# Holding back weights and second-batch transposes while the first scale is made, and six points per chunk in blocks of 256

## The chip, the cores and the metric

The kernel runs on one core of a Trainium2 chip. TensorE (PE) multiplies, VectorE (DVE) and ScalarE (ACT) work on tiles, GpSimd (POOL) does small side work, and SyncE (SP) issues nearly all transfers. The metric is the device time of one launch in microseconds (us), lower is better.

## The reference

Masked attention over 4 batches, 8 heads, 576 positions and head size 64, then two gated feed-forward layers over the 2304 tokens (512 wide, 1536 hidden). Heads 0 to 3 see the last 32 positions ("local"), heads 4 to 7 every 32nd earlier position ("strided").

```
attn = softmax(where(mask, q @ k.T / 8, -1e9)) @ v
x  = attn.transpose(0, 2, 1, 3).reshape(2304, 512)
xn = x / sqrt(mean(x * x, -1) + 1e-6) * rms_g        # layer 1 only
y  = (silu(xn @ w_gate) * (xn @ w_val)) @ w_out      # layer 1
out = (silu(y @ w2_gate) * (y @ w2_val)) @ w2_out    # layer 2
```

## The kernel before

**Products.** Each feed-forward operand is split into a high and a low part that TensorE multiplies in the type fp32r. A product of 128 by 128 weights with a token block is therefore three matmuls (high times high, high times low, low times high). The 1536 hidden columns are 12 chunks of 128. In layer 1 the first six chunks run over token blocks 0 (tokens 0 to 255), 1 (256 to 511), 2 (512 to 1023), 3 and 4; the last block of 256 tokens then runs all twelve chunks, and the others follow with chunks 6 to 11. Layer 2 goes the other way round. A chunk is a gate product (`b_g`), a value product (`b_v`), each 12 matmuls, and, two chunks later, the down product (`b_y`, 12 matmuls). While attention is still running there is one PSUM bank for the gate and one for the value (`GV`), so the gate product of a chunk can begin only when VectorE has read the one before it (`silu`, L670).

**Weights.** `weight_step` (L158) loads one of the three weights of a chunk (SP, L166), then rebuilds and splits it with three ScalarE and three VectorE instructions of 128x512: `dh` and `raw` on ScalarE (L175, L176), `raw` and `dh` on VectorE (L182, L183), `w` on ScalarE (L189) and `w` on VectorE (L194). The first six chunks have 18 weights. Three load buffers are shared with the loads of token blocks (`xraw`).

**Attention.** `Attention.batch` lists the steps of a batch: strided transposes (`strided_t`), scores with softmax, transposes of the softmax (`turn_step`), products with the values, local ones in the same way. From the second token block on they use two PSUM banks, `a0` and `a1`, in turn: a step's TensorE instructions wait until the bank's last reader on ScalarE or VectorE has finished.

**Normalising.** `rms_step(b, part)` scales a part of batch b: `pe1` sums squares on TensorE (`ones,ss`), `mean` runs on VectorE (L575) and then a power on GpSimd (L578), `diag` puts the result on a diagonal (`dg`, L583), `bc` spreads it over the partitions with TensorE (`dg,ones`), `post` scales x on VectorE (L594) and `store` writes x to DRAM. Batch 0's first part (256 tokens) is block 0: `split_x` (L693, L694) makes its high and low parts from SBUF. All later blocks come back from DRAM (`xraw`, L653) before their split. Block 2 needs the first part of batch 1.

**What sets the order.** One list of weight steps and one of attention steps are drawn from at "points" (`point`, L121), which stand between matmuls. At each point every active step moves on by one phase, and a new one starts when enough of its pace has gathered. In the start stage (up to batch 0's first part) there are only points; afterwards `proj` has points after its first and third quarter, `gate` one after each half and `down` two in layer 1: eight per chunk. A scheduler then places the instructions of each engine by priority; each engine executes its own in that order.

Of the kernel before, what the change touches and what calls it, by code (L numbers as in the profile page):

```python
# [8 lines left out]
F32 = mybir.dt.float32  # L9
# [3 lines left out]
ALU = mybir.AluOpType  # L13
# [8 lines left out]
PRIO_W = -150  # L22
# [3 lines left out]
def attn_ffn_ffn(ctx: ExitStack, tc: tile.TileContext, q, k, v, w1g, w1v, w1o, rms_g, w2g, w2v, w2o, out):  # L26
    nc = tc.nc
# [54 lines left out]
    last = {}  # L82
    active = []
    steps = []
    wq = []
    state = {"start": True, "rest": False, "kind": ""}

    def phase(st, prio=None):
        prio = st.prio if prio is None else prio
        with tc.high_priority(offset=0 if state["start"] and prio == PRIO_A else prio):  # L90
            state["kind"] = st.kind
            st.pop(0)()
            state["kind"] = ""

    def advance():
        for st in list(active):
            phase(st)
            if not st:
                active.remove(st)
# [21 lines left out]
    def point():  # L121
        advance()
        for nm, src in (("dec", wq), ("att", steps)):
            have[nm] = min(have[nm] + pace[nm], 2.0)
            while have[nm] >= 1.0 and src and src[0].ready():
                have[nm] -= 1.0
                start(src.pop(0))
# [80 lines left out]
    class Attention:  # L208
# [154 lines left out]
        def strided_t(self, b, which, part, last):  # L363
            cell = {}
            n = (126, 108, 108)[part]
            m = 64 if part == 2 else 128

            def pe():
                src = self.ld[b, 1][which]
                cell["t"] = tp = self.abank()  # L370
                for h in range(HH):
                    turned(tp[:m, n * h:n * h + n], src[:n, h, 128 * part:128 * part + m], self.ident[:n, :n])

            def post():
                o = (0, 504, 936)[part]
                copy(self.eng(), self.qk_tile(b, 1, which)[:m, o:o + 4 * n], cell["t"][:m, 0:4 * n])
                self.count(b, 1)
                if last:
                    self.load(b, 0)
                    if b == 0:  # L380
                        self.load_v(0, 0)

            return Step([pe, post])

        def softmax_step(self, ready, key, qn, kn, mks, mms):

# [171 lines left out]
        def rms_step(self, b, part):  # L558
            cell = {}
            o, w = parts(b)[part]  # L560
            tiles = [(j, min(128, w - j)) for j in range(0, w, 128)]
            nt = len(tiles)

            def pe1():
                cell["m"] = mp = self.abank()
                for i, (j, n) in enumerate(tiles):
                    product(mp[:n, i:i + 1], self.ss[b][:, o + j:o + j + n], self.ones[:, 0:1], start=True, stop=True)

            def mean():
                mp = cell["m"]  # L570
                m = self.p1.tile([128, 32], F32, tag="mean", name="mean")
                nc.gpsimd.memset(m, 1.0)
                for n in sorted({n for _, n in tiles}):
                    i0, i1 = [i for i, t in enumerate(tiles) if t[1] == n][0], [i for i, t in enumerate(tiles) if t[1] == n][-1] + 1
                    nc.vector.tensor_scalar(out=m[:n, i0:i1], in0=mp[:n, i0:i1], scalar1=1.0 / DM, scalar2=1e-6,  # L575
                                            op0=ALU.mult, op1=ALU.add)
                cell["r"] = r = self.p1.tile([128, 32], F32, tag="rstd", name="rstd")
                nc.gpsimd.tensor_tensor(out=r[:, :nt], in0=m[:, :nt], in1=self.expo[:, :nt], op=ALU.pow)  # L578

            def diag():  # L580
                cell["d"] = dg = self.p2.tile([128, 4, 128], F32, tag="e", name="dg", bufs=4).rearrange("p a k -> p (a k)")
                for i, (j, n) in enumerate(tiles):
                    nc.vector.tensor_scalar(out=dg[:n, j:j + n], in0=self.ident[:n, :n],  # L583
                                            scalar1=cell["r"][:n, i:i + 1], scalar2=None, op0=ALU.mult)

            def bc():
                cell["t"] = t = self.abank()
                for j, n in tiles:
                    product(t[:, j:j + n], self.ones[:n, :], cell["d"][:n, j:j + n], start=True, stop=True)

            def post():
                for c in range(KC):
                    x = self.x[b, c // 2][:, c % 2, o:o + w]
                    nc.vector.scalar_tensor_tensor(out=x, in0=x, scalar=self.gcol[:, c:c + 1], in1=cell["t"][:, :w],  # L594
                                                   op0=ALU.mult, op1=ALU.mult)

            def store():
                d = dp.tile([128, KC, w], F32, name=f"x_d{b}_{part}")
                for half in range(2):
                    nc.sync.dma_start(out=d[:, 2 * half:2 * half + 2, :], in_=self.x[b, half][:, :, o:o + w])  # L600
                x_d.append((b * S + o, w, d))
                self.done.add((b, part))

            return Step([wait] * 3 + [pe1, mean, diag] + [wait] * 1 + [bc, post, store], lambda: (b, part + 1) in self.sq and (not part or (b, 0) in self.done and not state["start"]), PRIO_R, "r")
# [57 lines left out]
    def ins_of(r):  # L662
        return getattr(r, "ins", r)
# [19 lines left out]
    @ahead  # L683
    def split_x(si):
        m, t0, n = segs[si][:3]
        xs = []
        x = xraw.pop((m, t0), None)
        p, w = pools[si % 2]
        for c in range(KC):
            xc = (x[c // 2] if x is not None else att.x[0, c // 2])[:, c % 2, :n]  # L690
            xh = p.tile([128, w], F32R, tag=f"xh{c}", name="xh")
            xl = p.tile([128, w], F32R, tag=f"xl{c}", name="xl")
            nc.scalar.copy(out=xh[:, :n], in_=xc)  # L693
            nc.vector.tensor_tensor(out=xl[:, :n], in0=xc, in1=xh[:, :n].bitcast(F32), op=ALU.subtract)  # L694
            xs.append((xh, xl))
        return xs

    def proj(pst, n, wtile, xs):
        for kk in range(KC):
            xh, xl = xs[kk]  # L700
            hi, lo = wtile[:, 0, kk * 128:kk * 128 + 128], wtile[:, 1, kk * 128:kk * 128 + 128]
            for a, b_, f, l in ((hi, xh, kk == 0, False), (hi, xl, False, False), (lo, xh, False, kk == KC - 1)):
                product(pst[:, :n], a, b_[:, :n], start=f, stop=l)
            if kk % 2 == 0:
                point()

    def gate(m, c, n, xs):
# [108 lines left out]
    waiting = []  # L816
    with tc.high_priority(offset=PRIO_R):
        xs_of = {0: split_x(0)}
    for _ in range(6):
        point()  # L820

# [17 lines left out]
    for si, (m, t0, n, c0, c1) in enumerate(segs):  # L839
        nxt = segs[si + 1] if si + 1 < len(segs) else None  # L840
        loaded = False
        pace["att"] = 0.6 if si < 2 else 1.2
        state["rest"] = si > TURN1
        pace["dec"] = 0.3 if si in (TURN1, TURN2) else 0.25
        xs = xs_of.pop(si)
# [59 lines left out]
```

## Time and profile before

| | us |
|---|---|
| median of 3 runs (1060.06 to 1067.89) | 1060.79 |
| profiled execution, time | 1059.67 |
| profiled execution, span | 1057.9 |
| PE busy / DVE busy / ACT busy / POOL busy | 1023.6 / 456.1 / 432.4 / 59.1 |

The profiled execution's time is 1.8 us more than its span. TensorE is busy for 97% of the span, so time can only come from the 34 us in which it is idle, from stretches where its granted clock is 1.2 instead of 2.4 GHz, and from waits that the busy time hides. In the page's forty slices the granted clock is at nine tenths or more in all but the second and the third.

### The profile page before, as it was taken

How to read it: one execution, taken by the hardware profiler on the slowest of the kernel's cores; microseconds unless marked ns; L12 is line 12 of the kernel's file. 1: busy time of each engine (PE TensorE's matmuls, PEld its weight loads, DVE VectorE, ACT ScalarE, POOL GpSimd, SP SyncE). 2: the span in 40 equal slices, each digit the busy share in tenths (PEclk: the TensorE clock that was granted, in tenths of full speed). 3: DMA queues.
4: the chain of work that ended last, by engine and by line, in shares of the span. 5: the costliest groups of instructions: out<-in, count | busy, mean ns of one | idle time of the engine just before them, and what ended most of it. 6: DMA issues, size and time to landing. Idle time of an engine off the chain costs nothing.

```text
span 1057.9 us, 14777 instructions
## 1 busy us (share of the span) xinstructions
PE 1023.6 (97%) x5624; PEld 865.8 (82%) x5624; DVE 456.1 (43%) x1104; ACT 432.4 (41%) x1046; POOL 59.1 (6%) x83
## 2 busy tenths in 40 slices
PE   5878999999999999999999999999999999999998
PEld 4667998787788899888888898888888888888887
DVE  3788364463447563751322785222224322222212
ACT  5988655465436463631211674212114322212111
POOL 3212112021000000000000000000000000000000
PEclk9759999999999999999999999999999999999999
DMA  7684161250135451741202474111103203020202
GB/s 194 186 229 141 40 188 46 77 155 2 41 110 186 142 169 39 216 142 54 99 21 80 140 229 160 40 40 40 40 1 120 80 1 99 11 80 1 80 1 90
DMA packets 100704, 100.71 MB, mean 95 GB/s; under 512 B 39445, under 2 KB 84701, under 8 KB 100633
## 3 DMA queue, kind: packets, MB, share of 16 engines
q1 hardware_dynamic: 100440, 99.49, 30.1%
q8 instruction: 44, 0.72, 0.3%
q0 software_dynamic: 192, 0.28, 0.1%
q14 instruction: 28, 0.22, 0.1%
HBM read 77.73 MB, written 22.02 MB: 94 GB/s over the span
## 4 chain that ended last, share of the span: by engine, by line
PE 89%; DVE 4%; DMA 3%; ACT 1%; SPq 1%; issue 1%; POOL 1%; DVEq 0%; POOLq 0%
PE b_y L66 28%; PE b_a L66 27%; PE b_v L66 16%; PE b_g L66 16%; PE b_a L69 2%; DMA raw<-in_moe_w_val_dram 1%; DVE e L399 1%; SPq L265 1%; DVE dh L183 1%; DMA raw<-in_moe_w_gate_dram 1%; DVE raw L182 1%; DMA kn<-in_k_dram 0%; DVE w L194 0%; DVE x L594 0%; DMA xraw<-y_d 0%
## 5 line engine op out<-in xcount | busy, mean ns | idle before, releaser
L66 PE MATMUL b_a<-xh,w 128*128 128x512 f32 (+1 forms) x816 | 234.8, 364 | 0.0
L66 PE MATMUL b_g<-xh,w 128*128 128x512 f32 (+1 forms) x600 | 182.1, 364 | 0.0
L66 PE MATMUL b_v<-xh,w 128*128 128x512 f32 (+1 forms) x600 | 180.9, 362 | 0.0
L66 PEld LDWEIGHTS b_a<-xh,w 128*128 128x128 f32 x816 | 147.9, 189 | 24.6
L680 ACT CAST hh<-sg 128x512 fp32r<-128x512 f32 (+1 forms) x126 | 70.3, 558 | 204.2 <-DVE sg L679 189.5
L66 PE MATMUL b_y<-hh,w 128*128 128x512 f32 (+1 forms) x528 | 153.0, 355 | 0.0
L66 PE MATMUL b_a<-xl,w 128*128 128x512 f32 (+1 forms) x408 | 148.5, 364 | 0.0
L66 PE MATMUL b_y<-w,hh 128*128 128x512 f32 x432 | 133.3, 390 | 0.0
L66 PEld LDWEIGHTS b_g<-xh,w 128*128 128x128 f32 x600 | 109.8, 190 | 17.1 <-issue 0.2
L66 PEld LDWEIGHTS b_v<-xh,w 128*128 128x128 f32 x600 | 108.9, 189 | 16.4
L66 PE MATMUL b_g<-xl,w 128*128 128x512 f32 (+1 forms) x300 | 107.1, 357 | 0.1
L66 PEld LDWEIGHTS b_y<-hh,w 128*128 128x128 f32 x528 | 95.0, 189 | 14.5 <-issue 0.7
L66 PE MATMUL b_v<-xl,w 128*128 128x512 f32 (+1 forms) x300 | 106.5, 355 | 0.0
L679 DVE TENSOR_TENSOR sg<-sg,b_v 128x512 f32<-128x512 f32 (+1 forms) x51 | 31.8, 623 | 162.6 <-PE b_v L66 162.4
L679 DVE TENSOR_TENSOR sg<-sg,b_a 128x512 f32<-128x512 f32 (+1 forms) x51 | 31.8, 623 | 157.8 <-PE b_a L66 157.7
L681 DVE TENSOR_TENSOR hl<-sg,hh 128x512 fp32r<-128x512 f32 (+1 forms) x126 | 79.3, 630 | 47.0 <-ACT hh L680 46.5
L66 PEld LDWEIGHTS b_y<-w,hh 128*128 128x128 f32 x432 | 80.4, 188 | 16.2
L66 PE MATMUL b_y<-hl,w 128*128 128x512 f32 (+1 forms) x264 | 92.6, 351 | 0.0
L66 PEld LDWEIGHTS b_a<-xl,w 128*128 128x128 f32 x408 | 77.0, 189 | 12.4
L672 ACT ACTIVATE sg<-b_a 128x512 f32<-128x512 f32 (+1 forms) x51 | 27.9, 547 | 140.9 <-PE b_a L66 140.7
L66 PE MATMUL b_y<-w,hl 128*128 128x512 f32 x216 | 84.0, 389 | 0.0
L672 ACT ACTIVATE sg<-b_g 128x512 f32<-128x512 f32 (+1 forms) x51 | 28.0, 548 | 120.8 <-PE b_g L66 120.7
(121 smaller groups left out, 1242.5 us busy)
## 6 DMA issues: line engine op xcount, KB each, us to landing
raw<-in_moe_w_gate_dram SPq DMA_DIRECT2D x24, 512.0 KB
raw<-in_moe_w_val_dram SPq DMA_DIRECT2D x24, 512.0 KB
raw<-in_moe_w_out_dram SPq DMA_DIRECT2D x24, 512.0 KB
xraw<-y_d SPq DMA_DIRECT2D x14, 512.0 KB
part<-ob SPq DMA_DIRECT2D x26, 256.0 KB
ob<-part SPq DMA_DIRECT2D x26, 256.0 KB
out_dram<-ob SPq DMA_DIRECT2D x18, 256.0 KB
y_d<-ob SPq DMA_DIRECT2D x16, 256.0 KB
```

The source lines that it names most:

```text
L66: traced(nc.tensor.matmul(out_, a, b_, start=start, stop=stop))
L69: traced(nc.tensor.transpose(out_, a, one))
L182: nc.vector.scalar_tensor_tensor(out=r, in0=cell["hw"], scalar=0x80000000, in1=r, op0=ALU.bitwise_and, op1=ALU.bitwise_or)
L183: nc.vector.scalar_tensor_tensor(out=h, in0=h, scalar=3, in1=r, op0=ALU.logical_shift_left, op1=ALU.bitwise_or)
L265: engs[h].dma_start(out=t[0:108, h].rearrange("p (g d) -> p g d", d=D), in_=s)
L399: r = nc.vector.tensor_tensor_reduce(out=e[:qn, i, :kn], in0=sp[:qn, i, :kn], in1=mk[:qn, :kn], scale=-0.125, scalar=3.0e38, op0=ALU.add, ...
L672: last["act"] = ins_of(nc.scalar.activation(out=s[:, :n], in_=pg[:, :n], func=AF.Silu))
L679: nc.vector.tensor_tensor(out=s[:, :n], in0=s[:, :n], in1=pv[:, :n], op=ALU.mult)
L680: last["act"] = ins_of(nc.scalar.copy(out=hh[:, :n], in_=s[:, :n]))
L681: last["dve"] = ins_of(nc.vector.tensor_tensor(out=hl[:, :n], in0=s[:, :n], in1=hh[:, :n].bitcast(F32), op=ALU.subtract))
```

## The change

Five edits. (1) While batch 0's first scale is being made, from its `pe1` to `split_x` of block 0, `hold` keeps weight steps from starting and from moving on. (2) The strided transposes of batch 1 become ready only when that part is done. (3) The first product after the start stage is ordered after the last one of `rms_step`. (4) Weight instructions of VectorE and ScalarE are placed behind the last split of block 0. (5) In blocks of 256 tokens `proj` has one point, after its second quarter, instead of two: a chunk then has six points (layer 1). The pace of attention in blocks 0 and 1 goes from 0.6 to 0.7 per point: 4.2 steps a chunk instead of 4.8. The pace of weights per point stays.

```diff
@@ state, advance, point @@
-    state = {"start": True, "rest": False, "kind": ""}
+    state = {"start": True, "hold": False, "rest": False, "kind": ""}
...
         for st in list(active):
+            if state["hold"] and st.prio == PRIO_W:
+                continue
             phase(st)
...
         for nm, src in (("dec", wq), ("att", steps)):
+            if state["hold"] and nm == "dec":
+                continue
@@ strided_t @@
-            return Step([pe, post])
+            return Step([pe, post], lambda: b != 1 or (0, 0) in self.done)
@@ rms_step, pe1 @@
+                if (b, part) == (0, 0):
+                    state["hold"] = True
@@ split_x @@
-            nc.scalar.copy(out=xh[:, :n], in_=xc)
-            nc.vector.tensor_tensor(out=xl[:, :n], in0=xc, in1=xh[:, :n].bitcast(F32), op=ALU.subtract)
+            ra = nc.scalar.copy(out=xh[:, :n], in_=xc)
+            rd = nc.vector.tensor_tensor(out=xl[:, :n], in0=xc, in1=xh[:, :n].bitcast(F32), op=ALU.subtract)
+            if si == 0:
+                last["act"], last["dve"] = ins_of(ra), ins_of(rd)
@@ proj @@
-            if kk % 2 == 0:
+            if kk in ((0, 2) if n > 256 else (1,)):
                 point()
@@ after the start stage @@
         xs_of = {0: split_x(0)}
+    state["hold"] = False
+    last["pe", None] = last["pe", "r"]
...
-        pace["att"] = 0.6 if si < 2 else 1.2
+        pace["att"] = 0.7 if si < 2 else 1.2
```

**TensorE, the first broadcast of the scale** (`dg,ones`) and the first transposes of batch 1 (`qn_482`, `kn_488`), as the difference of the two orders:

```order
 L66 MATMUL b_y_789<-ones,ss 128x1 x2
 L66 MATMUL b_a_809<-pT,vl_223 64x64 x4
+L66 MATMUL b_g<-dg,ones 128x128 x2
 L69 MATMUL b_a_860<-ident,qn_482 128x126 x4
 L69 MATMUL b_a_867<-ident,kn_488 128x126 x4
-L66 MATMUL b_g<-dg,ones 128x128 x2
 L69 MATMUL b_a_874<-ident,qn_482 128x108 x4
 L66 MATMUL b_a_879<-ones,ss 128x1 x2
```

The broadcast moved ahead of two groups of transposes. All six groups still stand ahead of the first gate product.

**VectorE, from the last squares to the second `mean`, before** (line 594 scales x, 694 splits it, 182, 183 and 194 are weight instructions):

```order
L555 TENSOR_TENSOR ss<-ss,sq 128x320
L183 SCALAR_TENSOR_TENSOR dh<-dh,raw 128x512
L594 SCALAR_TENSOR_TENSOR x_744<-x_744,gcol,b_g 128x256 x2
L594 SCALAR_TENSOR_TENSOR x_406<-x_406,gcol,b_g 128x256 x2
L182 SCALAR_TENSOR_TENSOR raw<-raw 128x512
L194 TENSOR_TENSOR w_3_1_500<-dh,w_3_1_500 128x512
L575 TENSOR_SCALAR mean<-b_a_879 64x1
L575 TENSOR_SCALAR mean<-b_a_879 128x2
```

The same place now (the line numbers of the changed kernel are 4 to 6 higher):

```order
L559 TENSOR_TENSOR ss<-ss,sq 128x320
L600 SCALAR_TENSOR_TENSOR x_744<-x_744,gcol,b_g 128x256 x2
L600 SCALAR_TENSOR_TENSOR x_406<-x_406,gcol,b_g 128x256 x2
L187 SCALAR_TENSOR_TENSOR dh<-dh,raw 128x512
L186 SCALAR_TENSOR_TENSOR raw<-raw 128x512
L700 TENSOR_TENSOR xl<-x_744,xh 128x256 x2
L700 TENSOR_TENSOR xl<-x_406,xh 128x256
L186 SCALAR_TENSOR_TENSOR raw<-raw 128x512
L187 SCALAR_TENSOR_TENSOR dh<-dh,raw 128x512
L581 TENSOR_SCALAR mean<-b_a_879 64x1
L581 TENSOR_SCALAR mean<-b_a_879 128x2
L700 TENSOR_TENSOR xl<-x_406,xh 128x256
```

One weight instruction moved from ahead of the scaling to behind it; the second `mean` now has four weight instructions and three splits between the scaling and itself, where it had two weight instructions.

**TensorE, the broadcast for block 2** (batch 1's first part) in block 1, before, where it stands between chunk 2 and the down product of chunk 0:

```order
L66 MATMUL b_v<-xl,w_2_1_435 128x256
L66 MATMUL b_v<-xh,w_2_1_435 128x256
L66 MATMUL b_a_1799<-dg,ones 128x128 x3
L66 MATMUL b_a_1799<-dg,ones 128x64
L66 MATMUL b_y_1804<-hh,w_0_2_281 128x256
```

and now, between the gate and the value product of chunk 4:

```order
L66 MATMUL b_g<-xl,w_4_0_556 128x256
L66 MATMUL b_g<-xh,w_4_0_556 128x256
L66 MATMUL b_a_1877<-dg,ones 128x128 x3
L66 MATMUL b_a_1877<-dg,ones 128x64
L66 MATMUL b_v<-xh,w_4_1_592 128x256
```

It moved back by nearly two of the six chunks of block 1. Between it and block 2's first product there are now 60 matmuls of 256 columns, six groups of transposes and batch 1's second broadcast.

## Rows read from the trace of the kernel before

**Rows 1.** The page's first line: the span of the profiled execution.

```profile
span 1057.9 us, 14777 instructions
```

**Rows 2.** Windows: start:end, length; busy PE, PEld, DVE, ACT, POOL; granted clock; DMA.

```profile
60.00:80.00 20.00, 17.44 (x100) 15.30 (x99) 18.70 (x57) 16.00 (x41) 4.08 (x4) 0.64 0.93 246
80.00:100.00 20.00, 16.15 (x132) 14.50 (x131) 17.91 (x60) 18.84 (x61) 6.93 (x6) 1.00 0.43 135
140.00:200.00 60.00, 59.12 (x470) 49.97 (x469) 28.85 (x134) 38.06 (x133) 11.25 (x13) 1.00 0.35 105
200.00:320.00 120.00, 119.51 (x706) 96.62 (x705) 57.22 (x187) 56.98 (x165) 14.10 (x18) 1.00 0.27 80
320.00:1057.00 737.00, 733.32 (x3572) 621.08 (x3570) 279.75 (x458) 235.69 (x428) 0.00 (x0) 1.00 0.26 85
```

**Rows 3.** Timeline of PE, 83 to 99: in brackets the idle time before.

```profile
83.43 0.65 PE L69 MATMUL b_a<-ident,e 126*126 126x126 f32 x4 [1.04 <-POOL e L425]
...
91.26 0.66 PE L69 MATMUL b_a<-ident,kn 128*128 128x128 f32 x4 [0.49 <-ACT x L76]
...
94.52 0.66 PE L69 MATMUL b_a<-ident,qn 128*128 128x128 f32 x4 [1.54 <-DVE qT L78]
...
98.18 0.33 PE L69 MATMUL b_a<-ident,qn 64*128 64x64 f32 x2 [0.78 <-DVE qT L78]
```

**Rows 4.** Timeline of PE, the first gate products and what stands before.

```profile
68.77 0.90 PE L69 MATMUL b_a<-ident,qn 108*64 108x108 f32 x4 [0.21 <-DVE mean L575]
...
70.39 0.56 PE L66 MATMUL b_g<-xh,w 128*128 128x256 f32 x1
...
72.46 1.71 PE L66 MATMUL b_a<-dg,ones 128*128 128x128 f32 x6
...
76.34 1.11 PE L66 MATMUL b_a<-kT,qT 64*126 64x126 f32 x8
```

**Rows 5.** Timeline of VectorE (DVE), 65 to 84.

```profile
65.03 0.69 DVE L183 SCALAR_TENSOR_TENSOR dh<-dh,raw 128x512 uint32<-128x512 uint32 x1
...
65.64 1.65 DVE L594 SCALAR_TENSOR_TENSOR x<-x,gcol,b_g 128x256 f32<-128x256 f32 x4
...
68.41 0.21 DVE L575 TENSOR_SCALAR mean<-b_a 64x1 f32<-64x1 f32 x2
...
70.42 0.74 DVE L694 TENSOR_TENSOR xl<-x,xh 128x256 fp32r<-128x256 f32 x2
...
71.92 0.64 DVE L583 TENSOR_SCALAR dg<-ident,rstd 128x128 f32<-128x128 f32 x3 [0.76 <-POOL rstd L578]
...
74.28 1.91 DVE L594 SCALAR_TENSOR_TENSOR x<-x,gcol,b_a 128x320 f32<-128x320 f32 x4
...
83.58 0.42 DVE L670 SCALAR_TENSOR_TENSOR sg<-sg,b_g 128x256 f32<-128x256 f32 x1
```

**Rows 6.** Timeline of GpSimd (POOL): two powers of the same shape.

```profile
68.77 3.12 POOL L578 TENSOR_TENSOR rstd<-mean,expo 128x3 f32<-128x3 f32 x1 [7.09 <-DVE mean L575]
...
206.40 0.86 POOL L578 TENSOR_TENSOR rstd<-mean,expo 128x3 f32<-128x3 f32 x1 [14.89 <-DVE mean L575]
```

**Rows 7.** Windows: the stretch up to block 0's last weight.

```profile
60.50:98.80 38.30, 31.89 (x215) 28.13 (x212) 34.92 (x113) 33.72 (x98) 11.01 (x10) 0.82 0.71 199
```

**Rows 8.** Timeline of VectorE: the last two weights of chunk 5.

```profile
98.16 1.29 DVE L194 TENSOR_TENSOR w<-dh,w 128x512 fp32r<-128x512 f32 x2
```

**Rows 9.** Chain of waits: start us, us, what: twelve products of 256 columns.

```profile
131.06 1.44 PE b_y L66 x12
```

**Rows 10.** Timeline of VectorE: two scalings, for blocks 2 and 3.

```profile
138.03 2.45 DVE L594 SCALAR_TENSOR_TENSOR x<-x,gcol,b_a 128x448 f32<-128x448 f32 x4 [0.58 <-PE b_a L66]
...
211.02 2.19 DVE L594 SCALAR_TENSOR_TENSOR x<-x,gcol,b_a 128x384 f32<-128x384 f32 x4
```

**Rows 11.** Timeline of ScalarE (ACT): the splits that follow them.

```profile
146.86 1.14 ACT L693 CAST xh<-xraw 128x512 fp32r<-128x512 f32 x2 [1.69 <-DMA xraw<-x_d]
...
217.93 1.14 ACT L693 CAST xh<-xraw 128x512 fp32r<-128x512 f32 x2 [0.85 <-DMA xraw<-x_d]
```

## The prediction

> **What bounds the kernel now.** I read the page first, then windows over stages, then TensorE's timeline where the windows leave it idle, and last the engines that it waits for there. The span is 1057.9 us [rows 1]. From 320 us to the end TensorE is idle for 3.7 us of 737 (737.00 less 733.32), from 200 to 320 for 0.49 of 120, from 140 to 200 for 0.88 of 60 [rows 2]: there the kernel is TensorE's own work, which the change leaves as it is. What an order can win lies between 60 and 100 us. There TensorE is idle for 2.56 and 3.85 us of two times 20, and its granted clock is 0.64 in the first of the two (a mix of the 1.2 and the 2.4 GHz level) [rows 2]. In the second the idle time is four gaps of 1.04, 0.49, 1.54 and 0.78 us [rows 3], 3.85 together. All four stand before a transpose of attention, whose operand or bank comes late from GpSimd, ScalarE or VectorE. The reader should see next that VectorE is busy for 34.92 of the 38.3 us up to the last weight of the first six chunks [rows 7]: in this stretch the bound is VectorE's queue, in its order, and TensorE waits for it.
>
> **The change part by part.**
>
> *The scale.* The broadcast now stands ahead of two groups of transposes, but the scaling of x on VectorE still comes behind the same squares and weight products; only one weight instruction (0.61 us, the step from 65.03 to 65.64) leaves the place ahead of it [rows 5]. So the scaling starts at 65.03 instead of 65.64, 0.6 us earlier, and nothing more is won on this path.
>
> *The second mean.* What VectorE puts between that scaling and the second `mean` grows: before, 2.77 us (65.64 to 68.41), namely the scaling and two weight instructions [rows 5]. Now it is the scaling (2.77 less two times 0.61, so 1.55), four weight instructions (2.44) and three splits of 0.37 (half of the 0.74 at 70.42), 1.11 [rows 5]: 5.10 us. The mean comes at 65.03 + 5.10 = 70.1 instead of 68.4, 1.7 us later. TensorE's fifth group of transposes waited for just this mean (0.21 us at 68.77), since it takes over its bank, and the first gate product followed at 70.39 [rows 4]. All transposes still stand ahead of it, so it starts at about 72.1. The edit that holds the weights back thus delays the gate by 1.7 us, by way of a bank.
>
> *The second scale.* It needs the power on GpSimd behind that mean. At 68.77 the power took 3.12 us, the same shape at 206.40 took 0.86 [rows 6]. At 68.77 VectorE ran on until 71.16 (70.42 + 0.74) and then waited 0.76 us for the power [rows 5]: it ended 0.73 us after VectorE's last instruction. I take that as the price: power done 0.73 us after VectorE pauses. Now a split and two weight products (1.6 us) follow the mean (70.1 + 0.2), so VectorE pauses at 71.9 and goes on at 72.6. The Trainium skill, GPSIMD Engine Reference, section Specifications, says that GpSimd shares its SBUF interfaces with VectorE and contends with VectorE instructions that have two SBUF inputs; by that rule, which speaks against placing such products behind the mean, the sum is the one above, and by a flat 3.12 us the second scale would come at 73.4 and the whole stretch 0.8 us later. The rows agree with the rule, as far as one power can.
>
> From 72.6 VectorE has the diagonal (0.64), four weight instructions (2.44), the gate's product (0.42), another weight instruction (0.61) and the second scaling (1.91): done at 78.6 [rows 5]. TensorE needs nine gate matmuls in 2.07 us (70.39 to 72.46), so twelve in 2.8, and 3.9 us (72.46 to 76.34) for broadcast, first scores and six matmuls: it reaches the second scores at 78.8 instead of 76.34 [rows 4], with three matmuls more behind it (0.36, at 1.44 for twelve [rows 9]). It is 2.1 us behind, without a new wait.
>
> *Weights ahead of the gate's bank.* By the tanh product of chunk 1, VectorE has now done 20 weight instructions since the first mean; before it had done 15 (counted in its order). That product stood at 83.58 [rows 5]; five more instructions are 3.05 us, so it comes at about 87, and TensorE, which may not start the gate of chunk 2 before, loses about 1 us. That is a loan: 7 of the 27 instructions are left then, where 12 were.
>
> *Spacing.* The first gap (1.04) goes, as the first transposed softmax now stands twelve matmuls later. Of the other three, 2.81 us [rows 3], I expect most to go, for fewer weight instructions and fewer steps stand in VectorE's queue there. Sum to 100 us: 2.1 + 1.0 - 1.04 - 2.5 = -0.4. The ends: -3.85 (all gaps go and no debt appears) and +3.1 (the debt stays). I take the middle, since VectorE has to do the same weights before its last one, which now as before lies between the tanh products of chunks 2 and 3. Before, it ended at 99.4 (98.16 + 1.29) [rows 8].
>
> *Steps moved to later blocks.* 4.2 instead of 4.8 steps a chunk (TensorE has 23 groups of attention in blocks 0 and 1 each, before 28), and block 3 gets the rest. Their matmuls take the same time anywhere. The idle time that could go is 0.88 us, what could come is as small; I take 0.
>
> *Block 2's input.* Its broadcast moves from chunk 2 to chunk 4 of block 1. TensorE then has 60 matmuls (7.2 us [rows 9]) and six groups of transposes (up to 0.66 each [rows 3]) before block 2. The way through DRAM took 8.8 us from the scaling to the first split (138.03 to 146.86) for block 2, and 6.9 us (211.02 to 217.93) for block 3 [rows 10, 11]. ScalarE stands at that split for the transfer, with copies behind it that free the attention banks: the next bank is free two casts (1.14) and a copy (about as long as one cast, 0.57) later, 10.5 or 8.6 us after the scaling. TensorE asks for it after 54 matmuls and five groups, 6.5 to 9.8 us, 8.2 in the middle. The wait is 0 to 4.0 us; by the second way, and the middle, 0.4. I take 0.5, because the loads of values that ran up to the first store are long done now. Blocks 3 and 4 also lose a chunk of cover, but theirs is of 512 columns, twice as long: 0.
>
> *Other blocks of 256.* Fewer points there also mean fewer weight phases: in the last block of layer 1, 1.8 weights a chunk instead of 2.4. The six that it must still fetch become free by chunk 3 and are wanted from chunk 10; six take 3.3 chunks. Covered, 0; if not, it would show as idle time after 320 us, where there is none to speak of now [rows 2].
>
> **The sum.** -0.4 + 0.5 + 0 = +0.1 on the profiled execution's 1059.67 us: **1059.8**. The median of the runs shown is 1.1 us above that execution; both are within what follows.
>
> **The rivals.** (a) *Spacing wins outright*: VectorE catches up at once, all four gaps go, and the late gate costs nothing, because the clock rises no later and the debt is paid within chunk 1. For it: the gaps are TensorE's only ones in the stretch, and each step now has more matmuls ahead of it. Against: the later mean and the 20 instructions. 1059.67 - 3.85 = 1055.8. (b) *VectorE's debt stays*: the gate of chunk 2 waits for its bank, and the weights do not give it back, because VectorE was busy for 34.92 of 38.3 us and has no room [rows 7]. It decides when the tanh product of chunk 1 comes later than about 87 us. 2.1 + 1.0 - 1.04 + 0.5 and one gap of 0.5 left: 1062.7, slower. (c) *Block 2 waits for its input*: the way of 8.8 us is the right one; it decides when the first split starts over 6.5 us after the scaling. 2.3 instead of 0.5: 1061.6. (d) *The change does not do what it says*: held weights move only behind the first scaling, so the scale comes no earlier. This is part of the forecast already; alone it would give 1059.7 with all the old gaps.
>
> **How the numbers follow.** Forecast 0.42, rival (a) 0.25, (b) 0.15, (c) 0.10, (d) 0.05, something not seen 0.03. The forecast's own range is 1058 to 1062, the profiled execution's and the median's reading both in it. The range reaches to (a) less 0.88 us of idle time later, and to (b) with the 1.1 us of the median on top: 1055.0 to 1064.0, which leaves about 2 in 10 out. A measurement of this kernel tells about 1% (10.6 us) from no change. No case comes to that: all idle time from 60 to 320 us is under 8 us [rows 2]. So within 1% 0.96, faster by over 1% 0.02, slower 0.02.
>
> **What would show it.** In the changed profile: the second mean near 70 and the first gate product near 72 (70.39 before); the power near 71 to 72.6; a wait of TensorE for the gate's bank near 87; at most one of the four gaps left up to 100; the last weight of chunk 5 done within 1 us of 99.4; at the end of block 1 a short idle time of TensorE before the second broadcast, released by ScalarE's copy of keys. The forecast is wrong if the gate starts at or before 70.4, if the last weight moves by over 2 us, or if TensorE idles by over 2 us at the end of block 1.

## The result and the profile after

The changed kernel takes 1073.58 us (median of 9 runs, 1066.82 to 1079.34), the kernel before 1064.44 (9 runs beside them, 1060.06 to 1067.89): ratio 1.0082, 95% interval 1.0056 to 1.0107. The forecast was 1059.8 in a range of 1055.0 to 1064.0: the change makes the kernel slower by 0.8%, and the time lies outside the range. The profiled execution of the changed kernel took 1073.92 us.

Its span and its windows answer to [rows 1] and [rows 2], in the same columns:

```profile
span 1072.1 us, 14771 instructions
```

```profile
60.00:80.00 20.00, 14.32 (x83) 12.58 (x83) 18.29 (x48) 15.58 (x33) 2.87 (x4) 0.67 0.90 235
80.00:100.00 20.00, 17.69 (x128) 15.90 (x128) 18.73 (x70) 18.16 (x66) 7.68 (x6) 0.91 0.46 146
140.00:200.00 60.00, 56.23 (x398) 48.15 (x397) 30.51 (x133) 32.92 (x117) 11.46 (x13) 0.97 0.36 103
200.00:320.00 120.00, 117.02 (x738) 93.22 (x737) 50.42 (x182) 56.52 (x172) 15.45 (x20) 0.96 0.24 67
320.00:1071.00 751.00, 747.21 (x3633) 632.12 (x3631) 293.28 (x481) 243.86 (x439) 0.00 (x0) 1.00 0.26 87
```

Behind 320 us nothing changed (3.79 us idle). Between 140 and 320 us, where TensorE had stood for 1.37 us at a clock of 1.00, it now stands for 6.75 and the clock falls to 0.97 and 0.96. The timeline of TensorE names the places, with the idle time in brackets:

```profile
78.98 1.11 PE L66 MATMUL b_a<-kT,qT 64*126 64x126 f32 x8 [2.48 <-DVE x L600]
...
94.50 0.66 PE L69 MATMUL b_a<-ident,qn 128*128 128x128 f32 x4 [0.45 <-ACT pT L76]
...
99.85 0.66 PE L69 MATMUL b_a<-ident,qn 128*128 128x128 f32 x4 [1.74 <-DVE qT L78]
...
157.32 0.49 PE L66 MATMUL b_a<-dg,ones 128*128 128x128 f32 x2 [1.02 <-ACT kT L76]
...
193.17 0.55 PE L69 MATMUL b_a<-ident,e 108*108 108x108 f32 x4 [1.35 <-issue]
...
194.98 0.59 PE L66 MATMUL b_a<-pT,vs 108*64 108x108 f32 x8 [0.55 <-DVE nb L403]
...
196.42 2.02 PE L66 MATMUL b_a<-kT,qT 128*128 128x96 f32 x8 [0.85 <-ACT pT L76]
...
240.53 3.06 PE L66 MATMUL b_a<-kT,qT 64*126 64x126 f32 x16 [2.49 <-ACT qT L76]
```

I call three of them A (79 us), B (193 to 196) and C (240). What stands behind B is read on VectorE, on ScalarE and on SP's queue:

```profile
181.10 0.42 DVE L78 COPY ob<-b_y 128x256 f32<-128x256 f32 x1
```

```profile
187.79 0.52 ACT L76 COPY pT<-b_a 108x432 f32<-108x432 f32 x1 [0.26 <-ACT e L412]
192.27 0.37 ACT L76 COPY ob<-b_y 128x256 f32<-128x256 f32 x1 [3.96 <-DMA part<-ob]
```

```profile
180.31 3.17 SPq L269 DMA_DIRECT2D qn<-in_q_dram  x4
...
184.11 3.05 SPq L269 DMA_DIRECT2D kn<-in_k_dram  x4
...
187.79 5.19 SPq L777 DMA_DIRECT2D part<-ob  x4
```

The products of block 1 are over. VectorE and ScalarE copy its four partial sums out in turn, into three buffers (`ob`, shared with `sg`), so the fourth copy needs a buffer whose store is done. The first copy ran at 181.10, but the stores stand on SP behind ten loads of the next batch (four, one, four and one) and start at 187.79. The fourth copy waits until 192.27, and ScalarE's copies for attention stand behind it. For the first of B's three waits the profile names no releaser ("issue"); that ScalarE is behind it too is shown by an experiment below. Before, five loads stood ahead of the store, the same copy waited for 2.05 us, and TensorE was idle for only 0.14 us in 185:200:

```profile
194.16 0.37 ACT L76 COPY ob<-b_y 128x256 f32<-128x256 f32 x1 [2.05 <-DMA part<-ob]
```

C is ScalarE too, at the splits of block 3's input:

```profile
236.19 1.14 ACT L699 CAST xh<-xraw 128x512 fp32r<-128x512 f32 x2 [1.87 <-DMA xraw<-x_d]
238.92 1.14 ACT L699 CAST xh<-xraw 128x512 fp32r<-128x512 f32 x2 [1.59 <-DMA xraw<-x_d]
239.97 0.51 ACT L76 COPY qT<-b_a 64x432 f32<-64x432 f32 x1
```

The qT copy that frees TensorE stands behind them. And behind B and C the granted clock is low, though TensorE is busy again (windows, clock behind the POOL column):

```profile
192.00:200.00 8.00, 5.44 (x28) 4.40 (x28) 3.72 (x21) 5.33 (x23) 0.83 (x1) 0.76 0.06 20
200.00:208.00 8.00, 8.00 (x41) 6.13 (x39) 1.84 (x10) 3.95 (x14) 1.28 (x2) 0.81 0.10 33
236.00:244.00 8.00, 5.51 (x29) 4.58 (x27) 5.17 (x17) 4.72 (x12) 0.00 (x0) 0.79 1.04 198
244.00:252.00 8.00, 8.00 (x37) 6.25 (x37) 4.50 (x32) 5.04 (x27) 2.48 (x3) 0.79 0.21 66
```

So B and C are each paid for twice. For ten of the profiled executions I add TensorE's idle time and the time lost to the 1.2 GHz level, taken as (1 - granted clock) x length over windows of 10 us. "8.0+8.4" is idle + lost, us:

| execution | time | 0-60 | 60-100 | 100-180 | 180-260 |
|---|---|---|---|---|---|
| before | 1059.67 | 22.0+11.5 | 6.4+7.3 | 0.3+0 | 1.1+0 |
| after | 1073.92 | 21.6+10.4 | 8.0+8.4 | 1.0+0 | 5.2+6.8 |
| hold alone | 1076.82 | 23.4+11.2 | 6.5+12.7 | 5.8+6.8 | 1.7+0 |
| six points at 0.7 alone | 1071.12 | 23.0+14.1 | 6.6+8.1 | 1.3+1.7 | 4.4+3.4 |
| change at 0.8 | 1062.00 | 22.4+10.1 | 7.0+12.1 | 0.5+0 | 0.1+0 |
| eight points at 0.525 | 1072.03 | 24.9+8.8 | 7.2+4.9 | 1.8+3.4 | 3.7+1.7 |
| 0.8, no hold | 1057.50 | 24.6+8.8 | 5.2+8.3 | 0.5+0 | 0.1+0 |
| change, stores off SP | 1064.36 | 26.1+8.4 | 8.1+8.6 | 1.7+0 | 2.0+0 |
| before, second | 1072.08 | 22.3+11.5 | 3.4+15.8 | 2.5+5.1 | 0.9+0 |
| before, third | 1076.18 | 23.6+11.8 | 3.1+17.2 | 3.8+3.4 | 2.2+1.7 |

From before to after these sums grow by 13.4 us up to 340 us, of a difference of 14.25; 11.0 of it lie in 180-260. This execution of before is a fast one, though: up to 340 us the second one has the same sum as after (62.0 us), with the loss in other places. What sets after apart is 180-260: 12.0 us, against 1.1, 0.9 and 3.9 in the three executions of before. The ratios leave out runs over 1.5% above the fastest of their kernel, and the third execution of before would be one of these.

### The profile page after: what moved, and what is told of

It is laid out like the page before. It is cut to its first block, busy times and chain, and to the rows that moved or that the text cites. A ratio compares the mean times of both kernels' runs of the same rounds, so it can differ in the third digit from the quotient of the medians.

```text
span 1072.1 us, 14771 instructions
## 1 busy us (share of the span) xinstructions
PE 1030.9 (96%) x5624; PEld 870.7 (81%) x5624; DVE 461.9 (43%) x1110; ACT 434.6 (41%) x1046; POOL 59.1 (6%) x83
## 4 chain that ended last, share of the span: by engine, by line
PE 84%; ACT 6%; DMA 5%; DVE 3%; SPq 1%; issue 1%; DVEq 0%; ACTq 0%
PE b_y L66 27%; PE b_a L66 26%; PE b_g L66 15%; PE b_v L66 15%; ACT e L412 2%; PE b_a L69 2%; DMA raw<-in_moe_w_gate_dram 1%; ACT raw L180 1%; DMA xraw<-x_d 1%; SPq L269 1%; DMA x_d<-x 1%; ACT dh L179 1%; DVE raw L186 1%; DMA ob<-part 1%; ACT w L193 1%
## 5 line engine op out<-in xcount | busy, mean ns | idle before, releaser
L66 PE MATMUL b_a<-xh,w 128*128 128x512 f32 (+1 forms) x800 | 230.2, 364 | 0.2 <-ACT xh L699 0.2
L66 PE MATMUL b_g<-xh,w 128*128 128x512 f32 (+1 forms) x608 | 184.8, 365 | 0.1
L66 PE MATMUL b_v<-xh,w 128*128 128x512 f32 (+1 forms) x608 | 183.2, 363 | 0.0
L66 PEld LDWEIGHTS b_a<-xh,w 128*128 128x128 f32 x800 | 144.9, 189 | 24.6 <-ACT xh L699 0.7
L66 PE MATMUL b_y<-hh,w 128*128 128x512 f32 (+1 forms) x528 | 156.6, 361 | 0.0
L66 PE MATMUL b_a<-xl,w 128*128 128x512 f32 (+1 forms) x400 | 145.6, 364 | 0.2 <-DVE xl L700 0.2
L66 PEld LDWEIGHTS b_a<-xl,w 128*128 128x128 f32 x400 | 75.5, 189 | 12.7 <-DVE xl L700 0.5
L678 ACT ACTIVATE sg<-b_g 128x512 f32<-128x512 f32 (+1 forms) x48 | 26.1, 544 | 133.8 <-PE b_g L66 133.8
L678 ACT ACTIVATE sg<-b_a 128x512 f32<-128x512 f32 (+1 forms) x48 | 26.1, 544 | 116.8 <-PE b_a L66 116.7
```

Of the source, the lines that this page charges most:

```text
L66: traced(nc.tensor.matmul(out_, a, b_, start=start, stop=stop))
L678: last["act"] = ins_of(nc.scalar.activation(out=s[:, :n], in_=pg[:, :n], func=AF.Silu))
```

## The experiments

My theory was that edit 5 (spacing and pace) makes B and C, and the hold (edits 1 to 4) only A; the rivals, that the hold makes all of it, or that not the steps per chunk but the places of the points decide. In the expectations "the third block's input" near 235 us is that of block 3; where one says "in block 1 and ... in block 2" of a pace, and for "the third" and "the fourth block" with a pace of 2.0, blocks are counted from one (blocks 0 to 3 here). The stalls near 91 to 98 us that one puts at "the end of block 1" lie in the middle of block 0, whose last gate product starts at 111.41; "edits 2 and 3" of the one on flowing weights are the second and third piece of the diff, both of edit (1).

**Hold alone, and spacing alone.** The first has edits 1 to 4; the second is

```diff
-            if kk % 2 == 0:
+            if kk in ((0, 2) if n > 256 else (1,)):
-        pace["att"] = 0.6 if si < 2 else 1.2
+        pace["att"] = 0.7 if si < 2 else 1.2
```

> The hold alone (weights and the second batch's first transposes wait for the first scale); points and pace are those of before. Theory, that the new spacing makes the loss and the hold only a small part of it: 1 to 4 us above before (about 1063), with the wait of the second scores for VectorE at 76 us and a clock under 0.65 just after it, but neither the 3.96 us wait of ScalarE for the output buffer at 192 us nor the 1.87 us wait for the block's input at 236 us; TensorE's granted clock in 140:200 and 200:260 us stays at 0.99 or more. Rival, that the hold makes all of it by shifting everything behind it: 10 to 15 us above before, with a clock of 0.93 or less in 200:260 us.

> Six points per chunk at 0.7 alone; no hold. Theory, that the spacing makes the loss: 8 to 11 us above before (about 1070), with ScalarE standing at the copy of block 1's partial sums near 190 us and at the third block's input near 235 us, TensorE idle over 2 us in each stretch and its clock between 0.50 and 0.75 for some 8 us after each. Rival, that the hold is at fault: within 2 us of before, clock 0.98 to 1.00 from 140 to 320 us.

Hold alone: 1073.64 us, ratio to before 1.0066 (1.0035 to 1.0097). Spacing alone: 1070.53, 1.0044 (1.0011 to 1.0077). Each is slower. The two prices make 1.1% together, where the change has 0.8%; the intervals are too wide to tell whether they add. The spacing cost half of what I expected, but it has B and C, without any hold (its timeline of TensorE; behind C the clock stayed up):

```profile
195.42 0.67 PE L69 MATMUL b_a<-ident,e 108*108 108x108 f32 x4 [2.11 <-issue]
...
240.94 1.69 PE L66 MATMUL b_a<-kT,qT 64*126 64x126 f32 x16 [1.95 <-ACT qT L76]
```

The hold has neither. It has A (2.26 us at 80.69), but it cost 7.8 us by the medians, where I had 1 to 4, and in its profiled execution another stall is the longest. In the middle of block 0 a copy of queries on VectorE stands behind late weights and the splits of block 1's input (timelines of TensorE and of VectorE, hold alone):

```profile
104.89 1.11 PE L69 MATMUL b_a<-ident,qn 128*128 128x128 f32 x4 [4.64 <-DVE qT L78]
```

```profile
101.08 0.68 DVE L187 SCALAR_TENSOR_TENSOR dh<-dh,raw 128x512 uint32<-128x512 uint32 x1
...
102.01 0.68 DVE L198 TENSOR_TENSOR w<-dh,w 128x512 fp32r<-128x512 f32 x1
...
104.14 0.69 DVE L78 COPY qT<-b_a 64x512 f32<-64x512 f32 x1
```

This wait is 1.74 us with hold and spacing (at 99.85 above), 2.64 with the spacing alone (at 99.50), and 1.54 to 2.22 in the three executions of before. That the spacing pays part of what the hold adds there is how I read these single executions; no run tests it. My split of the loss fell; that B and C belong to edit 5 stood.

**Pace or places.** The change with six points at 0.8, which gives the old 4.8 steps a chunk, and before with eight points at 0.525, which gives the change's 4.2:

```diff
-        pace["att"] = 0.7 if si < 2 else 1.2
+        pace["att"] = 0.8 if si < 2 else 1.2
```
```diff
-        pace["att"] = 0.6 if si < 2 else 1.2
+        pace["att"] = 0.525 if si < 2 else 1.2
```

> The change with a pace of 0.8 instead of 0.7: six points then make 4.8 attention steps per chunk, as eight points at 0.6 did. Theory, that it is the steps per chunk that let the scales come late against the blocks: the waits at 192 and 236 us shrink below 1 us of idle TensorE each, and the time is 2 to 5 us above before (the wait at 76 us stays), near 1063. Rival, that it is where the points stand and not how many steps they give: no nearer to before than the change is, 1070 to 1075.

> Before with a pace of 0.525 instead of 0.6: eight points then make 4.2 attention steps per chunk, as the change's six do at 0.7; everything else as before. Theory, that the steps per chunk decide: 5 to 11 us above before, with ScalarE's waits for the output buffer or for the third block's input of 1.5 us and more between 185 and 245 us and a lowered clock behind them. Rival, that the place of the points decides: within 2 us of before.

At 0.8: 1062.71 us, ratio 0.9968 (0.9941 to 0.9996). B and C are gone (the table), the 1.74 in block 0 too, and of the stalls named above only A is left; it is not 2 to 5 us slower than before but slightly faster. Eight points at 0.525: 1068.40, ratio 1.0012 (0.9979 to 1.0044). Its time can't be told from before, so the 5 to 11 us that I expected did not come; but its timeline of TensorE has stalls at both places, with the points where they were:

```profile
191.78 1.21 PE L66 MATMUL b_a<-kT,qT 128*128 128x96 f32 x8 [1.46 <-ACT pT L76]
```

```profile
231.11 0.59 PE L69 MATMUL b_a<-ident,kn 108*128 108x108 f32 x4 [1.91 <-ACT qT L76]
```

At 231 us ScalarE stood for 2.49 us at a split of block 3's input, as in C. At 191 us it stood at the fourth copy of block 1's sums, as in B, but for 1.10 us only, and no load was in the way: the stores started at 187.22, the loads were issued by 183.98. So the steps per chunk decide whether there are stalls at the two places, wherever the points stand. With eight points no run shows that they cost anything.

**The hold at 0.8.** First edits 1 to 4 are taken out of the change at 0.8; then only the hold of the weights (edit 1), and only the wait of the transposes (edit 2). Edits 3 and 4 stay in the last two:

> Six points per chunk at 0.8 and no hold: the change at 0.8 with edits 1 to 4 taken out. It prices the hold where nothing else is late. Theory, that the hold costs the wait of the second scores at 76 us and a lowered clock behind it: this kernel does without both (the second scores wait under 1 us, clock 0.95 or more in 80:100 us) and is 2 to 4 us faster than the change at 0.8, near 1060, 3 to 6 us below before. Rival, that the hold pays once the steps come fast enough: 2 us or more above the change at 0.8, 1064.5 or later.

```diff
-            if state["hold"] and st.prio == PRIO_W:
-                continue
...
-            if state["hold"] and nm == "dec":
-                continue
```

> The change at 0.8 with the hold of the weights taken out (edits 2 and 3 of the diff's list: the skip in the loop over active steps and the one for the queue of weight steps); the second batch's transposes still wait. Theory, that the wait of the second scores comes from the weight work that is kept back and then stands ahead of the second scaling on VectorE: without it the second scaling starts before 76 us (77.32 with both holds, 74.44 with neither), the second scores wait under 1 us, and the time is that of no hold at 0.8, 1059 to 1062. Rival, that the transposes that wait make it: second scaling after 76.5 us and 1062 to 1065, as with both.

```diff
-            return Step([pe, post], lambda: b != 1 or (0, 0) in self.done)
+            return Step([pe, post])
```

> The change at 0.8 with the wait of the second batch's transposes taken out; the weights are still held. Theory, that the weight hold makes the wait: second scaling after 76.5 us, second scores waiting 1.5 us or more, clock under 0.8 in 80:90 us, 1062 to 1065. Rival, that the transposes that wait make it: second scaling before 76 us, 1059 to 1062.

Without a hold 1060.30 us, ratio 0.9950 (0.9918 to 0.9983): the lowest time here. The lines of A, with both holds and with none (VectorE's second scaling, then TensorE's second scores):

```profile
77.32 1.92 DVE L600 SCALAR_TENSOR_TENSOR x<-x,gcol,b_a 128x320 f32<-128x320 f32 x4
```

```profile
79.39 1.11 PE L66 MATMUL b_a<-kT,qT 64*126 64x126 f32 x8 [2.19 <-DVE x L600]
```

```profile
74.44 1.91 DVE L594 SCALAR_TENSOR_TENSOR x<-x,gcol,b_a 128x320 f32<-128x320 f32 x4
```

```profile
76.50 1.11 PE L66 MATMUL b_a<-kT,qT 64*126 64x126 f32 x8 [0.64 <-DVE x L594]
```

The halves: only the transposes wait, 1063.98 (0.9979, 0.9952 to 1.0007), second scores waiting 3.09 us; only the weights wait, 1064.79 (0.9970, 0.9943 to 0.9997), 1.63 us. My theory that the hold of the weights makes the wait fell with the first of them: either half alone puts the second scaling behind 77.6 us (78.25 and 77.65), and the halves don't add. Edits 3 and 4 are in both, and whether one of these makes A is untested. A is shown to come with edits 1 to 4 (1.27 us or more in every kernel with them or with half of them, 0.64 or less without); its price at 0.8 is 2.4 us between medians, with intervals that overlap, so it is not shown. The clock of 0.95 that I expected without a hold did not come either: it was 0.79 in 84:92, where the gate product of chunk 2 waited for 1.38 us for its bank.

**B by itself.** The change, with the stores of partial sums issued by GpSimd while attention lives:

```diff
-            nc.sync.dma_start(out=d, in_=ob[:, :w])
+            (nc.gpsimd if m == 1 and not final and att is not None else nc.sync).dma_start(out=d, in_=ob[:, :w])
```

> The change, with the stores of partial sums issued by GpSimd instead of SP as long as attention is alive. Theory, that ScalarE stands at 188 to 192 us because that store is queued on SP behind ten loads of the next batch: the store leaves within 2 us of the copy, ScalarE's 3.96 us wait shrinks to 2 us or less, TensorE's idle time in 180:220 us falls from 2.75 to under 1 us with a clock of 0.95 or more there, and the time is 3 to 6 us below the change, near 1069; the stall at 240 us stays. Rival, that the wait is for the transfer and not for the queue: no change in the wait, 1072 to 1076.

1068.07 us, ratio 1.0013 (0.9981 to 1.0045), where the change stood at 1.0082: B costs 5.5 us by the medians, 0.7% by the ratios. GpSimd's timeline has the first store right behind the first copy (181.87), ScalarE waits for 1.09 us, and TensorE is idle for 0.00 us in 180:220:

```profile
182.59 1.15 POOL L777 DMA_DIRECT2D part<-ob  x2 [7.09 <-DVE ob L78]
```

C is still there (2.00 us at 234.63). The Trainium skill, DMA: Bandwidth & Descriptors, section "Issuing engines are not separate DMA queues", says that issuing from several engines saves only the time on the issuing sequencer, usually small beside the DMA. The trace agrees on what is saved, but here it was not small: ten issues of 0.47 to 0.8 us, 7.4 us together, stood ahead of a store that ScalarE waited for.

**Other paces.** 0.9, and 0.8 in one of the two blocks:

```diff
+        pace["att"] = 0.9 if si < 2 else 1.2
```
```diff
+        pace["att"] = (0.7, 0.8)[si] if si < 2 else 1.2
```
```diff
+        pace["att"] = (0.8, 0.7)[si] if si < 2 else 1.2
```

> The change with a pace of 0.9: six points then make 5.4 attention steps per chunk, more than before's 4.8. Theory, that earlier scales only help where a block waits for its input: no stall over 1 us between 100 and 320 us, as at 0.8, so 1061 to 1064, the same as at 0.8 within 1.5 us. Rival, that more steps per chunk crowd VectorE and ScalarE in block 1: TensorE idles over 2 us more in 80:140 us, and the time is 1066 or more.

> The change with 0.7 in block 1 and 0.8 in block 2. Theory, that each stall comes from how late the attention steps of its own stretch stand against the blocks: only part is given back; block 1 as in the change, the waits near 192 and 236 us smaller but not gone, 1065 to 1070. Rival, that block 1 alone decides (its lag is carried on): as the change, 1072 or more. Second rival, that block 2 alone decides: as the change at 0.8, 1061 to 1064.

> The change with 0.8 in block 1 and 0.7 in block 2, the mirror of the kernel with 0.7 and 0.8. Theory, that the stalls at 192 and 240 us come from attention steps that are late by what both blocks together have lost: 0.8 in block 1 alone gives back part, one stall of the two is left with over 1.5 us of idle TensorE, 1066 to 1071. Rival, that block 1 alone decides: as the change at 0.8 throughout, 1062 to 1064, no idle stretch over 1 us between 140 and 260 us. Second rival, that any 0.7 is enough: 1072 or more.

0.9: 1069.09 us, 1.0042 (1.0020 to 1.0063). Neither theory: the collision of B comes one block earlier, where nine loads of values stand ahead of the store of block 0's sums; ScalarE and then TensorE wait for it.

```profile
144.87 0.37 ACT L76 COPY ob<-b_y 128x256 f32<-128x256 f32 x1 [7.69 <-DMA part<-ob]
```

```profile
145.29 0.38 PE L66 MATMUL b_y<-hh,w 128*128 128x256 f32 x1 [1.77 <-ACT ob L76]
```

0.7 then 0.8: 1071.63, 1.0049 (1.0025 to 1.0074); 0.8 then 0.7: 1071.94, 1.0044 (1.0013 to 1.0076). Both have stalls at the places of B and C (1.81 and 2.25 us; 0.78, 0.85 and 1.15, 1.26 us of idle time), so one block at 0.7 is enough for them. Both ratios lie between before and the change, and their intervals overlap that of the change, so whether part of the loss is given back is not shown. At the place of B the loads are not what the store waits for: with 0.7 then 0.8 it started at 187.31, 0.35 us behind the first copy's end, and ScalarE waited for 3.60 us, until 192.47. A store's own way, from its start to the end of the wait for it, is about 2.9 us in before (191.25 to 194.16), 4.5 in after and 5.2 here. So there are two ways to B: a queue ahead of the store, or copies so close together that the fourth comes before the first is stored. Whether a fourth buffer would cure both, no run tested. I read 0.8 as a place between two collisions, not as a better pace in itself.

**C by itself, and the best kernel with the other cure.** The stores on GpSimd, with a pace of 2.0 in block 2, and the kernel at 0.8 without a hold with its stores on GpSimd:

```diff
+        pace["att"] = 0.7 if si < 2 else 2.0 if si == 2 else 1.2
```

> The change with the stores of partial sums on GpSimd and a pace of 2.0 instead of 1.2 in the third block, so that the scales for the fourth block come half a chunk earlier. Theory, that the stalls at 192 and 240 us are two separate prices: the second goes too (TensorE idle in 220:260 us under 1 us in place of 2.0 to 2.5), and the time is 2 to 4 us below the kernel with the stores alone, 1064 to 1066, what is left over the change at 0.8 being the end of block 1. Rival, that attention steps put closer together in block 3 make waits of their own: TensorE idles 1.5 us or more in 190:240 us, 1067 or more.

> Six points at 0.8, no hold, and the stores of partial sums on GpSimd: the best kernel so far with the other cure added. Theory, that with 0.8 no store is waited for any more, so nothing is left to gain: within 1.5 us of the kernel without, 1059 to 1062. Rival, that the wait for the store still falls into some executions and widens the spread: 2 us or more below it and a smaller spread, 1058 or less.

The first did not get rid of C (1.22 us at 233.64, with a clock of 0.83 in 236:244), and was no faster than the change: 1073.58 us, 1.0094 (1.0061 to 1.0128). B is back too (2.11 us at 194.55; timelines of VectorE, GpSimd and ScalarE):

```profile
186.42 0.39 DVE L78 COPY ob<-b_y 128x256 f32<-128x256 f32 x1
```

```profile
186.67 0.83 POOL L429 TENSOR_TENSOR e<-e,rc 128x384 f32<-128x384 f32 x1 [11.13 <-DVE rc L423]
187.44 1.14 POOL L777 DMA_DIRECT2D part<-ob  x2
```

```profile
192.29 0.37 ACT L76 COPY ob<-b_y 128x256 f32<-128x256 f32 x1 [3.62 <-DMA part<-ob]
```

The normalisation on GpSimd holds the store up by at most 0.6 us (186.81 to 187.44); the store itself takes 4.9. What C costs by itself stays open. The second took 1061.31 us, 0.9960 (0.9932 to 0.9989): nothing more to gain, as the theory had it.

**The base.** Two more profiled executions of the kernel before:

> The kernel before, unchanged, for another profiled execution: the one the forecast was built on took 1059.67 us, its median here is 1064 to 1066. Theory, that its stalls at the end of block 1 (0.49, 1.54 and 0.78 us) and at 194 us are long enough in a common execution to draw the lower clock: this one takes 1063 or more, with a clock under 0.95 somewhere in 100:260 us. Rival, that the difference lies before 60 us, in loading: the windows from 60 us on are as they were, idle and lost clock within 1 us.

> The kernel before once more, as the run above: with three profiled executions the place where they differ can be told from chance. The same numbers are expected.

They took 1072.08 and 1076.18 us; the median of before beside the experiments was 1064.35 to 1066.70. The rival fell: idle and lost time before 60 us differ by under 2 us. The theory holds for half: 100:180 costs 7 us more in both (the table). A stall in the middle of block 0 is longer than in the first execution (2.21 and 2.22 us for 1.54), comes behind 100 us, and is followed by a lowered clock worth 1.7 us in the second and 3.4 in the third. Another 3.4 of the second lie in 160:168, behind two stalls of 0.58 and 0.41 us. The other half, 5.5 and 6.6 us in 60:100, is no stall: it is the clock in 76:92 us, where TensorE is hardly idle (windows of the first execution of before, then of the second; then the second's stall on TensorE's timeline):

```profile
76.00:84.00 8.00, 6.87 (x53) 5.90 (x52) 7.60 (x46) 6.89 (x33) 1.65 (x2) 1.00 0.94 283
84.00:92.00 8.00, 7.51 (x65) 6.76 (x64) 6.44 (x21) 8.00 (x26) 5.28 (x5) 1.00 0.31 105
```

```profile
76.00:84.00 8.00, 8.00 (x34) 7.14 (x34) 5.01 (x29) 4.89 (x21) 0.00 (x0) 0.50 0.87 247
84.00:92.00 8.00, 7.92 (x38) 6.99 (x37) 3.69 (x22) 5.52 (x22) 3.78 (x4) 0.52 0.27 94
```

```profile
100.86 0.66 PE L69 MATMUL b_a<-ident,qn 128*128 128x128 f32 x4 [2.21 <-DVE qT L78]
```

## Why the prediction was wrong, step by step

The rows of after for the stretch to 100 us, against [rows 4 to 6]:

```profile
64.64 1.65 DVE L600 SCALAR_TENSOR_TENSOR x<-x,gcol,b_g 128x256 f32<-128x256 f32 x4
...
69.62 0.21 DVE L581 TENSOR_SCALAR mean<-b_a 64x1 f32<-64x1 f32 x2
...
70.09 0.68 DVE L198 TENSOR_TENSOR w<-dh,w 128x512 fp32r<-128x512 f32 x1
...
76.92 1.92 DVE L600 SCALAR_TENSOR_TENSOR x<-x,gcol,b_a 128x320 f32<-128x320 f32 x4
```

```profile
69.98 1.51 POOL L584 TENSOR_TENSOR rstd<-mean,expo 128x3 f32<-128x3 f32 x1 [7.77 <-DVE mean L581]
```

```profile
71.28 0.56 PE L66 MATMUL b_g<-xh,w 128*128 128x256 f32 x1
```

- **The scale, the second mean, the gate:** right in kind. 64.64 (forecast 65.03), 69.62 (70.1), first gate product 71.28 (72.1, before 70.39).
- **The power:** right. It took 1.51 us and ended 0.72 us after VectorE's product at 70.09; the forecast took 0.73 after VectorE pauses. The flat 3.12 did not come. With the hold alone and at 0.8 it is again 1.51 us, ending 0.72 behind that product; in the three executions of before it is 3.12. This agrees with the Trainium skill, GPSIMD Engine Reference, section Specifications. But VectorE paused for 0.30 us only and ran its next product from 71.07 on, so part of the power lay beside a product again; how much of a pause it needs, the rows don't show.
- **The second scores "2.1 us behind, without a new wait":** wrong. The second scaling ended at 78.84 (78.6), but TensorE was there at 76.50, not 78.8: twelve gate matmuls took 2.42 us and what follows 2.80, where I had 2.8 and 3.9 from rows at a mixed clock. So there was a new wait, of 2.48.
- **Weights ahead of the gate's bank:** the product came at 87.41 (87), yet TensorE was not idle in 84:92: 0 instead of 1.0. (In the kernel at 0.8 without a hold there is such a wait, 1.38.) The last weight ended at 100.5, 1.1 later than before.
- **Spacing:** 3.85 us of gaps [rows 3] became 2.19; I had 0.31 left. Up to the tanh of chunk 3 the two profiled executions differ by 0.3 us (99.46 and 99.77), against a forecast of -0.4. That the sum comes out to here is luck: the second scores began 2.6 us late (2.1 in the sum), the bank cost 0 for 1.0, the gaps gave back 1.7 for 3.5, and TensorE was busy for 1.6 us less in 60:100 ([rows 2] and above), with work that was still to come. And the second execution of before has this tanh at 106.97, 7.5 us behind the first.
- **Block 2's input:** 1.02 us instead of 0.5; from the scaling (147.50) to the first split (155.71) 8.2 us, within its bounds.
- **"Steps moved to later blocks ... I take 0" and "Blocks 3 and 4 ... 0":** these are the steps that failed. I looked for idle time that matmuls make when they move, and found none; but the steps carry loads on SP and copies on ScalarE with them, and these met the store of block 1's sums (B) and the input of block 3 (C). Rival (c) had C's mechanism, one block too early; for B there was no rival, because I followed no queue of SP past the end of a block. In place of these zeros the runs show 0.7% for B alone, a stall at C whose price stays open, and a change that at 0.8, with 4.8 steps a chunk again, is no slower than before.
- **"No case comes to that: all idle time from 60 to 320 us is under 8 us":** wrong twice. New idle time can arise, and it is not the whole price: from before to after idle time grew by 6.6 us and lost clock by 6.8.
- **The sum was made on 1059.67 us:** the median of before is 4.8 us above it, and the three profiled executions spread over 16.5 us. Of the 13.8 us by which the forecast missed, 4.8 are this base and 9.1 the change, less the 0.1 that was forecast.
- **Other blocks of 256:** right, 0.
- **The signs:** none of the three that were to show the forecast wrong came (gate at 71.28, last weight 1.1 us later, 1.02 us at the end of block 1). The loss arose where I had set no sign.

## What to carry to other kernels

When an edit changes how many background steps fall into a unit of work, follow the queues that those steps carry (loads on SP, copies on ScalarE) to the next end of a block, and look there for an instruction that waits in order with others behind it. A store whose buffer somebody waits for should not be queued behind loads that nobody needs yet; and even at the head of its queue it took up to 5.2 us here, so count the buffers that are written meanwhile. And take the base of a sum from several profiled executions, since one can lie far from the median.

## What was not expected of the hardware

- A stall of TensorE can cost more than its length again. In the changed kernel idle times of 1.02 and 1.74 us left the clock at 1.00. The 2.48 us of A were followed by a lowered clock worth 1.7 us ((1 - 0.79) x 8), the 2.49 of C and the three short ones of B by one worth 3.4 each. Length alone does not decide: 2.00 us (stores off SP, 234.63) cost no clock, 1.63 us (eight points at 0.525, at 153.49) was followed by 0.70 in 152:160. Nor does the program: two stalls of 0.58 and 0.41 us were followed by 0.58 in 160:168 in the second execution of before; in the third the same two (0.58 and 0.38 us) left the clock at 1.00.
- The return of the clock behind nearly the same stalls (3.83, 1.97, 0.18 and 0.21 us between 54 and 69 us in the first execution of before; 3.94, 1.51, 0.17 and 0.21 in the second) varies by 15 us and more: 1.00 from 76 us in the first, 0.50 in 76:84 and 0.52 in 84:92 in the second, in which TensorE was busy 8.00 and 7.92 of 8 us. In 60:100 this loses 15.8 us in place of 7.3, of which 3.0 come back because the slower TensorE waits less. No run here shows what decides it.
